# A delta-rule attention and a softplus-erf MLP on one core: a new hand-over order of 3663 operations, and other engines for some copies

## The chip, the core and the metric

The kernel runs on one core of a Trainium2 chip. The metric is the device time of one execution in microseconds, lower is better. Three runs of the kernel before took 779.32, 781.75 and 782.74 us. The profile is of a fourth execution.

## What is computed

The first half is a recurrence over 768 steps with a state of 40 x 40 per head, for 4 x 8 heads. Its output, 3072 tokens of 320 numbers, goes through an MLP of width 2048. All is float32; the weights arrive as float64.

```python
for t in range(S):
    y[:, :, t] = np.einsum('bhd,bhde->bhe', rt, state)
    Sa = np.einsum('bhde,bhe->bhd', state, at)
    state_decay = state * wt[:, :, None, :] - np.einsum('bhd,bhe->bhde', Sa, bt)
    state = state_decay + np.einsum('bhd,bhe->bhde', vt, kt)
...
h = x @ w_in
sp = np.maximum(h, 0.0) + np.log1p(np.exp(-np.abs(h)))
g = h * erf(sp)
return (g @ w_out).astype(np.float32)
```

## The kernel before

The 768 steps are cut into 12 stages of 64, and a stage into two chunks of 32. Stages are counted from 0 here. Each stage has these parts, all heads side by side:

- `prep` (L416) multiplies up the decays w with scans on VectorE (DVE).
- `aphase` (L444), once per chunk: A (L466) multiplies keys by scaled keys, Am (L477) masks the product, and AD writes the part that has to be inverted to DRAM. bT (L485) transposes the keys.
- `tphase` (L490), once per stage: 28 short DVE operations (L512, L513) invert 16 x 16 blocks; TD and tb (both L373) carry the result through DRAM. W and DAD (both L531, 128 small matmuls each on the chip) make the off-diagonal blocks, with the copy Wm between them, and Tb (L538) adds their product into the tile `Tb`.
- `chain` (L540), once per chunk, carries the state on: Z (L571), copy zt, U (L582, which reads `Tb`), copy us, four copies zu of `Us` into `Vu` (L592), the transposes pmt (L599) and UT (L608), copy vtu, PQ (L618), the mask PQm (L621), and MY (M is L632, Y is L636), whose sum gives the new state (MT, L639) and the output (Ym, L641).
- the MLP follows a stage behind: `load_x` (L768) reads the output back and splits it into a high and a low half, mm1 (L802) multiplies by w_in, 8 matmuls to a group of 128 x 256, `unit` (L817) makes the activation on ScalarE (ACT) and DVE, and mm2 (L854) multiplies by w_out, 128 x 320. E and G (L844, L845) give the `h` that mm2 reads.

At the start, 190 warm-up matmuls (L413) write a tile that nobody reads, and `weights` (L700) turns float64 into float32 pairs (L719 to L737).

No loop fixes what runs when. The methods only list operations, each with the keys that it reads and writes, and `Plan.schedule` (L205) returns two tables that stand at the top of the file: `ORDER`, a permutation of the numbers 0 to 3662, and `ENGINES`, one letter for each operation (P TensorE, A ACT, V DVE, S SP, G GpSimd). Operations are handed over in that order, and each engine runs its own in the order handed over.

```python
        for o, e in zip(ops, self.engines):
            o["eng"] = CODE[e]
        return list(self.order)
...
                for i in order:
                    o = N.P.ops[i]
                    N.cur = i
                    o["fn"](o["eng"])
```

Only copies (`copy`, L365, with its lines L367 on ACT and L369 on DVE), fills and the zu copies (L592: ACT, DVE, or a DMA on SP's queue) have a choice of engine. All DMAs are issued in order on SP's queue.

Of the kernel before, what the change touches and what calls it, by code (L numbers as in the profile page):

```python
# [15 lines left out]
17 6 13 10 2 3 4 5 20 210 217 1 457 216 233 232 0 297 435 21 22 23 24 25 26 27 28 29 30 31 32 33 34 35 36 37 38 39 40 41 42 43 44 45 46 47 48 49 50 51  # L16
52 53 54 55 56 57 58 59 60 61 212 211 9 12 8 11 7 219 213 215 218 235 234 62 63 64 65 66 67 68 69 70 71 220 221 72 73 475 74 75 76 77 78 79 224 225
214 298 228 299 300 19 229 18 436 463 464 14 301 80 81 82 230 231 83 84 85 236 237 15 476 240 241 222 223 461 226 306 442 227 243 242 337 441 248 249
86 87 88 89 90 91 92 466 93 94 95 96 97 98 99 100 101 102 103 104 105 106 107 108 109 110 111 244 112 113 114 115 116 302 117 118 119 120 304 121 465
122 123 303 245 252 253 305 307 308 437 309 444 438 440 338 254 255 256 257 258 259 310 124 125 126 246 127 128 129 130 131 132 313 133 134 135 136  # L20
137 138 139 140 477 141 142 143 144 145 146 147 148 311 149 150 151 152 153 154 155 156 315 328 238 359 251 462 346 459 260 316 317 318 261 262 263
264 265 266 329 267 268 269 270 271 272 273 274 275 276 277 278 330 279 280 281 331 443 360 467 339 340 478 319 332 321 312 157 158 159 160 161 162
163 164 165 322 166 167 168 169 170 171 368 250 239 282 283 377 285 284 386 16 247 369 314 370 378 286 347 348 379 349 323 324 172 173 174 175 176 325
333 177 335 178 179 180 181 182 183 184 185 186 187 188 287 288 289 290 291 189 190 191 292 192 293 294 193 295 194 195 196 380 361 362 363 371 387
296 388 389 469 468 445 446 341 327 334 350 326 470 450 449 479 344 197 198 453 199 200 473 480 345 491 509 506 448 458 460 407 395 399 510 490 411
452 481 482 493 396 336 454 472 471 474 483 397 408 409 201 342 455 484 486 485 492 353 524 487 202 354 488 513 489 398 456 352 355 525 343 372 512
203 356 494 495 514 515 516 526 517 518 364 366 358 390 519 498 410 527 499 528 511 497 403 507 451 415 508 501 500 427 496 696 447 547 548 521 404
# [934 lines left out]
```

## Time and profile before

| | |
|---|---|
| median of 3 runs | 781.75 us (779.32 to 782.74) |
| profiled execution, its own time | 776.95 us |
| its span, first to last instruction | 775.2 us |
| granted TensorE clock, mean | 0.973 of full speed |
| busy: TensorE / DVE / ACT / GpSimd | 717.8 / 622.8 / 525.8 / 6.6 us |
| moved by DMA | 93.97 MB, 121 GB/s |
| warm-up matmuls (L413) within TensorE's busy time | 48.3 us |

TensorE's busy time holds matmuls; weight loads (PEld, 573.5 us) overlap them. Busy shares are an average over stages. In the waits of an engine, "issue" means that no semaphore explains the wait. The DMA queues are told by kind; those of kind instruction bring the engines' program, not data.

### The profile page before, as it was taken

To read this page: it belongs to the slowest core of one execution; us is meant where nothing else is said; L and a number is where in the kernel's file an instruction comes from. 1 tells how busy PE (TensorE), PEld (TensorE's weight loads), DVE (VectorE), ACT (ScalarE), POOL (GpSimd) and SP (SyncE) were. 2 spreads that over 40 slices of the span, in tenths; PEclk is the share of its full clock that TensorE was granted. 3 is DMA by queue.
4 is the path that set the end of the run, shared out by engine and by line. 5 is a ranking of instruction groups with operands and counts; after the bars stand their busy time and mean duration, and the time that the engine had idled before them with its cause. 6 is when DMAs were issued, how large, how long until landed. Compare 5 with 4: busy or idle time off the path is not lost.

```text
span 775.2 us, 30880 instructions
## 1 busy us (share of the span) xinstructions
PE 717.8 (93%) x13807; PEld 573.5 (74%) x13807; DVE 622.8 (80%) x1115; ACT 525.8 (68%) x739; POOL 6.6 (1%) x11
## 2 busy tenths in 40 slices
PE   9998788799989999999979989999999999998986
PEld 4556577577877787887867777788788887787863
DVE  7876887797887797888958967878988897678573
ACT  3324456747786697687957667787778885787791
POOL 3000000000000000000000000000000000000000
PEclk9999999999999999999989989999999999999998
DMA  7996776463464563645473662466545643521000
GB/s 193 240 211 189 191 188 150 92 144 97 104 158 91 142 155 68 158 123 115 97 154 75 130 152 62 103 164 150 113 107 125 148 105 94 103 61 41 16 18 21
DMA packets 172480, 93.97 MB, mean 121 GB/s; under 512 B 142484, under 2 KB 154132, under 8 KB 172340
## 3 DMA queue, kind: packets, MB, share of 16 engines
q1 hardware_dynamic: 172340, 91.93, 50.7%
q8 instruction: 110, 1.80, 1.0%
q14 instruction: 30, 0.25, 0.1%
HBM read 73.52 MB, written 14.16 MB: 113 GB/s over the span
## 4 chain that ended last, share of the span: by engine, by line
PE 78%; DVE 9%; issue 5%; DMA 4%; ACT 2%; SPq 1%; DVEq 0%; ACTq 0%
PE po L854 23%; PE ph L802 21%; PE ph L413 6%; PE pA L531 4%; PE my L632 4%; PE pA L466 4%; PE pQ L618 3%; PE my L582 3%; PE pQ L599 2%; PE pA L485 2%; PE my L571 2%; DMA Tb<-TD 2%; PE my L636 2%; PE pQ L608 1%; SPq L373 1%
## 5 line engine op out<-in xcount | busy, mean ns | idle before, releaser
L854 PE MATMUL po<-wo,h 128*128 128x320 f32 x768 | 242.8, 449 | 7.4 <-DVE h L845 6.8
L854 PEld LDWEIGHTS po<-wo,h 128*128 128x128 f32 x768 | 137.1, 193 | 52.3 <-DVE h L845 7.5
L810 ACT ACTIVATE l<-l 128x1024 f32<-128x1024 f32 x96 | 99.1, 1055 | 5.2 <-DVE nd L833 4.6
L802 PE MATMUL ph<-xh,wih 128*128 128x256 f32 x384 | 94.3, 327 | 1.3 <-issue 1.3
L802 PE MATMUL ph<-xh,wil 128*128 128x256 f32 x384 | 78.3, 285 | 0.5 <-issue 0.5
L802 PE MATMUL ph<-xl,wih 128*128 128x256 f32 x384 | 78.2, 286 | 0.0
L802 PEld LDWEIGHTS ph<-xh,wih 128*128 128x128 f32 x384 | 63.1, 194 | 9.8 <-issue 1.7
L367 ACT COPY h<-ph 128x512 f32<-128x512 f32 x74 | 42.7, 584 | 40.3 <-PE ph L802 35.3
L833 DVE TENSOR_TENSOR nd<-l,r 128x1024 f32<-128x1024 f32 x48 | 58.5, 1219 | 5.2 <-ACT r L810 3.6
L802 PEld LDWEIGHTS ph<-xh,wil 128*128 128x128 f32 x384 | 60.8, 194 | 1.4 <-issue 1.4
L802 PEld LDWEIGHTS ph<-xl,wih 128*128 128x128 f32 x384 | 60.6, 194 | 0.0
L834 DVE SCALAR_TENSOR_TENSOR r<-nd,r 128x1024 f32<-128x1024 f32 x48 | 58.4, 1217 | 0.5
L844 DVE TENSOR_TENSOR l<-l,r 128x1024 f32<-128x1024 f32 x48 | 58.2, 1218 | 0.7
L845 DVE SCALAR_TENSOR_TENSOR h<-l,h 128x1024 f32<-128x1024 f32 x48 | 58.3, 1219 | 0.6
L802 PE MATMUL ph<-xh,wir 128*128 128x256 f32 x192 | 54.9, 286 | 2.3 <-DVE xh L369 2.3
L802 PE MATMUL ph<-xl,wir 128*128 128x256 f32 x192 | 55.0, 286 | 0.6 <-issue 0.6
L810 ACT ACTIVATE l<-h 128x1024 f32<-128x1024 f32 x48 | 50.0, 1054 | 0.6 <-DVE h L369 0.2
L810 ACT ACTIVATE r<-l 128x1024 f32<-128x1024 f32 x48 | 49.3, 1052 | 1.6 <-DVE l L844 1.5
L632 PE MATMUL my<-Vu,sg 64*40 64x72 f32 x1536 | 46.4, 230 | 4.1 <-DVE Pr L641 1.4
L810 ACT ACTIVATE r<-r 128x1024 f32<-128x1024 f32 x48 | 49.6, 1056 | 0.4
L413 PE MATMUL ph<-d 104*128 104x512 bf16 x190 | 48.3, 396 | 1.6 <-DVE d L384 1.6
L632 PEld LDWEIGHTS my<-Vu,sg 64*40 64x40 f32 x1536 | 34.9, 115 | 18.2 <-DVE MT L639 4.1
(122 smaller groups left out, 1284.5 us busy)
## 6 DMA issues: line engine op xcount, KB each, us to landing
bk<-in_kba_e SPq DMA_DIRECT2D x48, 416.0 KB
vt<-in_rv_e SPq DMA_DIRECT2D x48, 240.0 KB
h<-in_moe_w_in SPq DMA_DIRECT2D x10, 512.0 KB
h<-in_moe_w_out SPq DMA_DIRECT2D x10, 512.0 KB
Pr<-in_w_e SPq DMA_DIRECT2D x12, 422.9 KB
Rt<-in_r_e SPq DMA_DIRECT2D x24, 208.0 KB
Zm<-in_v_s SPq DMA_DIRECT2D x24, 160.0 KB
Zs<-bk SPq DMA_DIRECT2D x48, 80.0 KB
```

Source lines behind the costliest of these rows:

```text
L367: self.nc.scalar.copy(o, i)
L413: P.add("warm", "PE", lambda e: nc.tensor.matmul(s.ph[1], s.d1[:, :128], s.d1[:, :512], start=True, stop=True), ["d1"], ["phw"], -1e3, 0.22)
L466: nc.tensor.matmul(pa[i % 2 * 64:i % 2 * 64 + 64, i // 4, i // 2 % 2], bk[:, i].rearrange("p a b -> p (a b)"), ab[:, :, i], start=True, st ...
L531: nc.tensor.matmul(pw[js, i, ts], l[js, i], r[js, i, ts], start=True, stop=True)
L632: nc.tensor.matmul(my[h * 64:h * 64 + 40, x, j], sg[xs, g, j, h], vu[xs, g * HQ + j // 2 * 2 + h, j % 2], start=True, stop=False)
L802: nc.tensor.matmul(ph[:, j * 256:j * 256 + 256], a[:k, fs], b[:k], start=(m == 0), stop=(m == 7))
L810: self.P.add(name, "ACT", lambda e: nc.scalar.activation(out=o, in_=i, **kw), rd, wr + ["act"], pr, 1.06)
L833: P.add("nd", [("DVE", 1.2)], lambda e, r=r, l=l, nd=nd: s.eng(e).tensor_tensor(out=nd, in0=l, in1=r, op=ALU.mult), kl + kr, kn, pr)
L834: P.add("rho", "DVE", lambda e, r=r, nd=nd: nc.vector.scalar_tensor_tensor(out=r, in0=nd, scalar=2 * C4, in1=r, op0=ALU.add, op1=ALU.mult) ...
L844: P.add("E", [("DVE", 1.2)], lambda e: s.eng(e).tensor_tensor(out=l, in0=l, in1=r, op=ALU.mult), kr, kl, pr)
L845: P.add("G", "DVE", lambda e: nc.vector.scalar_tensor_tensor(out=h, in0=l, scalar=-1.0, in1=h, op0=ALU.add, op1=ALU.mult), kl, kh, pr, 1.2)
L854: nc.tensor.matmul(po, h[:, bs], s.wo[:, f], start=(f == 0), stop=(f == 15))
```

## The change

Both tables are replaced. The list of operations, their functions and their dependencies stay as they are.

```diff
 ORDER = tuple(int(x) for x in """
-17 6 13 10 2 3 4 5 20 210 217 1 457 216 233 232 0 297 435 21 22 23 24 25 26 27 28 29 30 31 32 33 34 35 36 37 38 39 40 41 42 43 44 45 46 47 48 49 50 51
...
+2 4 3 17 6 7 9 10 12 15 8 5 20 210 1 217 0 216 232 297 435 233 337 457 306 21 22 23 24 25 26 27 28 29 30 31 32 33 475 34 35 36 37 38 39 40 41 42 43 44
...
 ENGINES = "".join("""
-SSVVVVGGGAGGAGAVVGAAPPPPPPPPPPPPPPPPPPPPPPPPPPPPPPPPPPPPPPPPPPPPPPPPPPPPPPPPPPPPPPPPPPPPPPPPPPPPPPPPPPPPPPPPPPPPPPPPPPPPPPPPPPPPPPPPPPPPPPPPPPPPPPPPPPPPPPPP
...
+SSVVVVGGVGGAGAAVVGAAPPPPPPPPPPPPPPPPPPPPPPPPPPPPPPPPPPPPPPPPPPPPPPPPPPPPPPPPPPPPPPPPPPPPPPPPPPPPPPPPPPPPPPPPPPPPPPPPPPPPPPPPPPPPPPPPPPPPPPPPPPPPPPPPPPPPPPPP
...
```

By the second table, the zu copies go from 65 on ACT, 24 on DVE and 7 on SP to 40, 41 and 15. The copies h of mm1's result (L367 on ACT, L369 on DVE) go from 74 and 22 to 80 and 16; the copies of x (`xh`) from 18 and 18 to 12 and 24; those of bT's result from 35 and 13 to 44 and 4. The rest moves by a few.

TensorE in stage 2, from W to the first U, before. `Ti` is W's operand and `Tb` that of DAD and U; a count at the end of a row is of the program's matmuls, and each of L531, L582 and L854 is two on the chip:

```order
L531 MATMUL pA<-Ti,Aw 32x16 x64
L854 MATMUL po_131<-wo,h 128x320 x3
L531 MATMUL pA<-Tb_76,Aw 32x16 x64
L854 MATMUL po_131<-wo,h 128x320
L854 MATMUL po_132<-wo,h 128x320
L466 MATMUL pA<-bk_86 64x2x32 x16
L582 MATMUL my<-zt,Tb_76 32x40 x32
```

The same place now:

```order
L531 MATMUL pA<-Ti,Aw 32x16 x48
L854 MATMUL po_131<-wo,h 128x320
L531 MATMUL pA<-Ti,Aw 32x16 x16
L854 MATMUL po_131<-wo,h 128x320
L531 MATMUL pA<-Tb_76,Aw 32x16 x48
L854 MATMUL po_131<-wo,h 128x320 x2
L531 MATMUL pA<-Tb_76,Aw 32x16 x16
L854 MATMUL po_132<-wo,h 128x320
L582 MATMUL my<-zt,Tb_76 32x40 x32
```

Four rows of L854 now stand inside W and DAD where three stood, and one stands between DAD and U where two stood and A (L466).

TensorE in stage 8, DAD and what follows it, before:

```order
L531 MATMUL pA<-Tb_76,Aw 32x16 x64
L854 MATMUL po_132<-wo,h 128x320
L466 MATMUL pA<-bk_86 64x2x32 x16
L854 MATMUL po_131<-wo,h 128x320
L582 MATMUL my<-zt,Tb_76 32x40 x32
```

DAD of the same stage now:

```order
L531 MATMUL pA<-Tb_76,Aw 32x16 x32
L802 MATMUL ph_129<-xh_0_122,wih_110 128x256
L802 MATMUL ph_129<-xh_1_123,wih_111 128x256
L802 MATMUL ph_129<-xh_2_124,wir 128x256
L802 MATMUL ph_129<-xl_0_125,wih_110 128x256
L802 MATMUL ph_129<-xl_1_126,wih_111 128x256
L802 MATMUL ph_129<-xl_2_127,wir 128x256
L802 MATMUL ph_129<-xh_0_122,wil_112 128x256
L802 MATMUL ph_129<-xh_1_123,wil_113 128x256
L854 MATMUL po_132<-wo,h 128x320 x2
L854 MATMUL po_131<-wo,h 128x320 x2
L531 MATMUL pA<-Tb_76,Aw 32x16 x32
```

A group of mm1 and four rows of mm2 now cut DAD in two halves.

SP's queue in stage 2, where a copy of `Us` into `Vu` is issued, before:

```order
L373 DMA AD_105<-Zs_68 32x16x32
L373 DMA bk_86<-in_kba_e 104x1024
L592 DMA Vu<-Us 32x8x40
L373 DMA xd<-Pr_80 40x4x64 x3
L373 DMA AD_105<-Zs_69 32x16x32 x2
```

In the same stage now:

```order
L373 DMA bk_87<-in_kba_e 104x1024
L373 DMA vt_93<-in_rv_e 40x2x768
L592 DMA Vu<-Us 32x8x40 x2
L373 DMA AD_105<-Zs_68 32x16x32 x2
L373 DMA out<-ob_128 64x320
```

Two such copies are issued one behind the other, and behind them on the queue stand the transfer of the next product to DRAM and a piece of the output.

## Rows read from the trace of the kernel before

**Rows 1.** The page: busy time by engine, and the chain's shares by engine.
```profile
PE 717.8 (93%) x13807; PEld 573.5 (74%) x13807; DVE 622.8 (80%) x1115; ACT 525.8 (68%) x739; POOL 6.6 (1%) x11
...
PE 78%; DVE 9%; issue 5%; DMA 4%; ACT 2%; SPq 1%; DVEq 0%; ACTq 0%
```
**Rows 2.** Waits of TensorE: line, releaser, us in total, times, longest us.
```profile
PE pA L531 <- issue: 17.9, 9, 3.9
PE po L854 <- DVE h L845: 6.8, 6, 2.2
PE my L582 <- issue: 5.3, 5, 2.1
...
PE pQ L608 <- ACT Us L367: 1.9, 3, 0.7
```
**Rows 3.** The page, DMA queues: packets, MB, share of 16 engines.
```profile
q8 instruction: 110, 1.80, 1.0%
```
**Rows 4.** Timeline of TensorE in stage 6: start us, us, instructions, idle before.
```profile
399.09 1.20 PE L531 MATMUL pA<-Tb,Aw 32*32 32x16 f32 x74 [3.91 <-issue]
...
404.35 0.96 PE L582 MATMUL my<-zt,Tb 32*32 32x40 f32 x42
406.15 0.41 PE L582 MATMUL my<-zt,Tb 32*32 32x40 f32 x22 [0.83 <-issue]
```
**Rows 5.** The chain that ended last, in order of time: start us, us, what.
```profile
56.90 3.10 issue
...
104.98 5.02 DMA Tb<-TD
...
115.61 2.73 issue
...
231.16 1.37 issue
...
395.18 3.91 issue
...
400.29 2.00 PE ph L802 x8
402.29 2.13 PE po L854 x4
...
432.84 4.85 PE po L854 x18
...
443.44 4.79 PE ph L802 x40
...
457.16 3.74 issue
...
518.98 1.27 issue
...
698.96 1.28 issue
```
**Rows 6.** Busy time in four stretches: us, engines, granted clock, DMA share, GB/s.
```profile
399.10:406.20 7.10, 6.27 (x132) 4.85 (x135) 2.78 (x3) 0.00 (x0) 0.00 (x0) 0.57 0.44 96
...
452.00:457.00 5.00, 5.00 (x221) 4.76 (x221) 4.81 (x4) 4.97 (x7) 0.00 (x0) 1.00 0.82 192
...
461.00:467.00 6.00, 6.00 (x159) 4.59 (x159) 3.46 (x4) 0.00 (x0) 0.00 (x0) 0.54 0.27 89
...
570.00:575.00 5.00, 4.46 (x196) 3.80 (x185) 4.10 (x4) 4.66 (x7) 0.00 (x0) 1.00 0.14 45
```
**Rows 7.** The tile Tb: its writer on DVE, ns min/median/max.
```profile
L538 DVE TENSOR_TENSOR Tb<-pA,Tb x12: 425/425/426, 60.4 to 685.5; 128x256 f32<-128x256 f32 x12
```
**Rows 8.** Line L592 on ACT, and the timeline from one such DMA to the first M.
```profile
L592 ACT COPY Vu<-Us x65: 453/457/462, 63.4 to 702.4; 32x320 f32<-32x320 f32 x65
...
191.90 0.63 SPq L592 DMA_DIRECT2D Vu<-Us  x1
...
196.20 0.34 PE L632 MATMUL my<-Vu,sg 64*40 64x72 f32 x8
```

More of the change, by code (lines that the diff above doesn't have):

```diff
@@ L156 @@
-PAPVPPVPVVPVVSSSSSSAVPPAPPVAVAAPVPVPAPPVPVVPVVSSSSSSSSVPVVSVVSVVSSVVAAAAAAAAVVVVAAAPPVPPAAPPAPPAAVVPPPPPPPPVVPPPPPPPPVSSVSSAAAAAAAAVVVVAAAPPVPPVAPPVPP
+SSVVVVGGVGGAGAAVVGAAPPPPPPPPPPPPPPPPPPPPPPPPPPPPPPPPPPPPPPPPPPPPPPPPPPPPPPPPPPPPPPPPPPPPPPPPPPPPPPPPPPPPPPPPPPPPPPPPPPPPPPPPPPPPPPPPPPPPPPPPPPPPPPPPPP
+PPPPPPPPPPPPPPPPPPPPPPPPPPPPPPPPPPPPPPPPPPPPPPPPPPPPPPPPPPPPSAVVVVSSVVPPSSVVSSPAPASSVVPPSSVVSSPAPASSSSAAVVVVVVVVVVVVVVVVVVVVVVVVVVVVSSSSVPPPPAPPPPVSVV
+VAPAPVSVVVAPAPASVVVAAAPVVPAVSVVVAPAPVSVVVAPAPASVVVAAAPAAPAVSVVVAPVPASVVVAPAPVSVVVAPVPASVVVAPAPASVVVSVVVSVVVSVVVSVVVSVVVSVVVSVVVSVVVSVVVSAVVVVSSVVPPSSV
@@ new lines @@
+VSSPAPASSSSSSAVPPVPPAAAAAPAPVPAPPVPVVPVVSSVVPPSSVVSSPAPASSSSSSAVPPAPPAAVAVPAPAPAPPVPVVPVVSSSSSSSSSSSSAAVVVVVVVVVVVVVVVVVVVVVVVVVVVVSSSSVPPPPAPPPPVSAVS
+AVSSVVPPAPPAAPPAPPAAAAAAAAAAVVVVAAAPPVPPVAPPAPPAAVVPPPPPPPPVVPPPPPPPPSAVVVVSSVVPPSSVVSSPAPVSSSSSSVVAPPVPPAVVAAPAPAPAPPVPVVPVVSSVVPPSSVVSSPAPASSSSSSVVP
+PAPPAVVAAPVPVPVPPVPVVPVVSSSSSSSSSSSSAAVVVVVVVVVVVVVVVVVVVVVVVVVVVVSSSSVPPPPAPPPPVSAVSVVSSAVAAAAAAAAVVVVAAAPPAPPAAPPAPPAAVVPPPPPPPPVVPPPPPPPPASSASSAAAA
+AAAAVVVVAAAPPAPPAAPPAPPAAVVPPPPPPPPVVPPPPPPPPSAVVVVSSVVPPSSVVSSPAPASSSSSSVAAPPAPPVVASSPAPAPVPPVPVVPVVSSVVPPSSVVSSPAPASSSSSSVAPPAPPAASSVPVPVPAPPVPVVPVV
@@ new lines @@
+SSSSSSSSSSSSAAVVVVVVVVVVVVVVVVVVVVVVVVVVVVSSSSVPPPPAPPPPVSVVSAVSSVVAAAAAAAAVVVVAAAPPVPPAAPPAPPAAVVPPPPPPPPVVPPPPPPPPVSSASSAAAAAAAAVVVVAAAPPAPPAAPPAPPA
+AVVPPPPPPPPVVPPPPPPPPSAVVVVSSVVPPSSVVSSPAPASSSSSSVAVPPAPPAAAVAPAPAPVPPVPVVPVVSSVVPPSSVVSSPAPASSSSSSVAPPAPPAAVAVPVPAPAPPVPVVPVVSSSSSSSSSSSSAAVVVVVVVVVV
+VVVVVVVVVVVVVVVVVVSSSSVPPPPAPPPPVSAVSAVSSVVAAAAAAAAVVVVAAAPPVPPAAPPAPPAAVVPPPPPPPPVVPPPPPPPPASSVSSAAAAAAAAVVVVAAAPPAPPAAPPAPPAAVVPPPPPPPPVVPPPPPPPPSAV
+VVVSSVVPPSSVVSSPAPASSSSSSVAVPPAPPAVAVSPVPAPAPPVPVVPVVSSVVPPSSVVSSPAPVSSSSSSAVPPAPPAVAVVPVPAPAPPVPVVPVVSSSSSSSSSSSSAAVVVVVVVVVVVVVVVVVVVVVVVVVVVVSSSSVP
@@ new lines @@
+PPPAPPPPVSVVSVVSSAVAAAAAAAAVVVVAAAPPVPPAAPPAPPAAVVPPPPPPPPVVPPPPPPPPASSASSAAAAAAAAVVVVAAAPPAPPAAPPAPPAAVVPPPPPPPPVVPPPPPPPPSAVVVVSSVVPPSSVVSSPAPASSSSS
+SVAAPPVPPAAVVAPAPVPAPPVPVVPVVSSVVPPSSVVSSPAPASSSSSSAVPPVPPAVAAAPVPAPAPPVPVVPVVSSSSSSSSSSSSAAVVVVVVVVVVVVVVVVVVVVVVVVVVVVSSSSVPPPPAPPPPVSVVSAVSSVVAAAAA
+AAAVVVVAAAPPAPPAAPPAPPVAVVPPPPPPPPVVPPPPPPPPASSVSSAAAAAAAAVVVVAAAPPAPPAAPPVPPAAVVPPPPPPPPVVPPPPPPPPSAVVVVSSVVPPSSVVSSPAPASSSSSSVAAPPAPPASVVSPAPVPAPPVP
+VVPVVSSVVPPSSVVSSPAPASSSSSSAVPPAPPAVVVSPAPAPAPPVPVVPVVSSSSSSSSSSSSAAVVVVVVVVVVVVVVVVVVVVVVVVVVVVSSSSVPPPPAPPPPVSVVSVVSSAVAAAAAAAAVVVVAAAPPAPPAAPPAPPAA
@@ new lines @@
+VVPPPPPPPPVVPPPPPPPPASSASSAAAAAAAAVVVVAAAPPVPPAAPPAPPAAVVPPPPPPPPVVPPPPPPPPSAVVVVSSVVPPSSVVSSPAPASSSSSSVVVPPAPPAVVAAPVPAPAPPVPVVPVVSSVVPPSSVVSSPAPASSS
+SSSVVPPAPPAVAVAPVPVPAPPVPVVPVVSSSSSSSSSSSSAAVVVVVVVVVVVVVVVVVVVVVVVVVVVVSSSSVPPPPAPPPPVSVVSVVSSVVAAAAAAAAVVVVAAAPPAPPAAPPAPPAAVVPPPPPPPPVVPPPPPPPPASSA
+SSAAAAAAAAVVVVAAAPPVPPAAPPAPPAAVVPPPPPPPPVVPPPPPPPPSAVVVVSSVVPPSSVVSSPAPASSSSSSVAAPPVPPASVSVPAPVPAPPVPVVPVVSSVVPPSSVVSSPAPVSSSSSSAAPPAPPVAVAVPAPAPAPPV
+PVVPVVSSSSSSSSSSSSAAVVVVVVVVVVVVVVVVVVVVVVVVVVVVSSSSVPPPPVPPPPVSVVSVVSSVVAAAAAAAAVVVVAAAPPAPPAAPPAPPAAVVPPPPPPPPVVPPPPPPPPASSASSAAAAAAAAVVVVAAAPPAPPAA
@@ new lines @@
+PPAPPAAVVPPPPPPPPVVPPPPPPPPSAVVVVSSVVPPSSVVSSPAPASSSSSSVAAPPVPPAAVSSPVPAPAPPVPVVPVVSSVVPPSSVVSSPAPASSSSSSVAPPAPPAVAVAPVPAPAPPVPVVPVVSSSSSSSSSSSSAAVVVV
+VVVVVVVVVVVVVVVVVVVVVVVVSSSSVPPPPAPPPPVSVVSAVSSVVAAAAAAAAVVVVAAAPPAPPAAPPAPPAAVVPPPPPPPPVVPPPPPPPPVSSASSAAAAAAAAVVVVAAAPPAPPAAPPAPPAAVVPPPPPPPPVVPPPPP
+PPPSAVVVVSSVVPPSSVVSSPVPASSSSSSVVAPPAPPAAAASPVPAPVPPVPVVPVVSSVVPPSSVVSSPAPASSSSSSVVPPAPPAASSAPAPAPAPPVPVVPVVSSSSSSSSSSSSAAVVVVVVVVVVVVVVVVVVVVVVVVVVVV
+SSSSVPPPPAPPPPVSVVSVVSSVVAAAAAAAAVVVVAAAPPAPPAAPPAPPAAVVPPPPPPPPVVPPPPPPPPVSSVSSAAAAAAAAVVVVAAAPPAPPVAPPVPPAAVVPPPPPPPPVVPPPPPPPPSSSSSSVAVPPAPPAVVVVPV
@@ L157 @@
+PVPAPPVPVVPVVSSSSSSVAPPAPPAAAVVPAPAPVPPVPVVPVVSSSSSSSSVPVVSVVSAVSSVVAAAAAAAAVVVVAAAPPVPPAAPPAPPAAVVPPPPPPPPVVPPPPPPPPVSSVSSAAAAAAAAVVVVAAAPPVPPVAPPVPP
 VAVVPPPPPPPPVVPPPPPPPPAAAAAAAAVVVVAAAVVPPPPPPPPVVPPPPPPPPASSASS
```

23 lines of the change are left out of this document (removed), and 228 rows, old and new, of the table ORDER.

## Prediction

> **What bounds the kernel now.** I read first the busy times and the chain that ended last. The reader is to see that TensorE is busy for 717.8 of 775.2 us and carries 78% of the chain [rows 1], so what matters is what stops TensorE. The chain's next shares are DVE with 9% and "issue" with 5%, and issue is time in which the engine waited for nothing that the profile shows.
>
> Then the waits of TensorE [rows 2]. The longest total is no dependency: L531 sat 17.9 us behind "issue", in 9 waits of up to 3.9 us, and L582 5.3 us in 5. All waits for VectorE's h at L845 are 6.8 us together. The table of DMA queues has one queue of kind instruction with 110 packets and 1.80 MB, about 16 kB each [rows 3]. TensorE runs 13807 matmuls and as many weight loads [rows 1], so one such packet serves about 251 instructions. The timeline shows the same grain: between the wait that ends at 399.09 and the one that ends at 406.15 stand 74, 8, 4 and 42 matmuls [rows 4, 5], 128 matmuls with their 128 weight loads, 256 instructions. So I read these waits as the end of a block of 256 instructions whose successor has not arrived. They fall on L531 because its matmuls are the smallest: 74 take 1.20 us [rows 4], while 18 of L854 take 4.85 us and 40 of L802 take 4.79 us [rows 5].
>
> A page speaks against such waits. The Trainium skill, "Runtime: NRT & Kernel Launch", section "Instruction fetch mechanics", has blocks of 256 instructions fetched during the one before, and calls the crossing "mostly hidden". The size agrees with the trace, the hiding doesn't at the tiny matmuls; by that rule the change would gain nothing.
>
> Two more things decide the size of a wait. In the 5 us before the 3.74 us wait at 457.16 the DMA engines were busy at 0.82; around the same place of stage 9, 570 to 575, they were at 0.14 and TensorE worked 4.46 of the 5 us [rows 5, 6]. So a load seems late when data fills the engines. And the granted clock falls behind a long wait: 0.57 over the 7.1 us from 399.1 and 0.54 over the 6 us from 461 [rows 6]; 8 matmuls of L802 then take 2.00 us and 4 of L854 2.13 us [rows 5], where the full-clock rows give 8 x 4.79/40 = 0.96 and 4 x 4.85/18 = 1.08.
>
> **The change, part by part.** Every transfer, matmul and vector operation is still there, so TensorE's own work is unchanged. What moves is the filler between the small matmuls. One group of L802 (8 rows of the order) costs 0.96 us. One row of L854 is two matmuls on the chip, 2 x 4.85/18 = 0.54 us. I counted both in all stages 1 to 11.
>
> (a) Between the first W and the last DAD (both L531) there stood 25 groups of L802 and 14 rows of L854, 24.0 + 7.6 = 31.6 us. Now there are 27 and 31, 25.9 + 16.7 = 42.6 us, 1.0 us more per stage. A wait shrinks at most by the filler added. Stage 1 waits 2.73 us and gains one group: 0.96. Stage 3 waits 1.37 and gains one row: 0.54. Stage 6 waits 3.91 and gains one group and one row: 1.50. Stage 8 waits 1.27 and gains three rows, 1.62: all 1.27. The waits of L531 besides the six listed make 17.9 - (3.10 + 2.73 + 1.37 + 3.91 + 3.74 + 1.27) = 1.8 us [rows 2, 5], in stages that gain at least as much: 1.8. Together 6.1. Stage 7 goes the other way: of its three groups two now stand inside W, ahead of the block that runs out, so its 3.74 us may grow by 2 x 0.96 = 1.9. Stage 0 has warm-up matmuls as filler; I leave it at nothing. Net 4.2 us off, bounds 2 (one of the gains more fails) and 6.1 (stage 7 does not grow).
>
> (b) The filler came mostly from behind DAD. Before the second U (L582) there stood 20 rows of L854, now 10: 5.4 us less. There L538 must add DAD's product to Tb, 425 ns each [rows 7], so the one row that is left (0.54) just hides it. But U has block ends of its own, 5.3 us [rows 2]. Bounds 0 (hidden) and 5.4 (every microsecond reappears); I take 2: of those waits one shows in stage 6 right after DAD, at 406.15 [rows 4], and it can grow by the 0.96 that left there; one more stage like it makes 2.
>
> (c) The half clock cost (2.00 - 0.96) + (2.13 - 1.08) = 2.1 us in stage 6, and I price stage 7 alike. Bounds 0 and 4.2; I take 2, since only stage 6's wait is cut.
>
> (d) Block ends elsewhere, such as the 1.28 us at 698.96 [rows 5], get a little more or less filler. At 698.96 one group of L802 now stands before the end. Bounds -1 and +3; I take 1.5 off.
>
> (e) Copies change engine. Of L592's 96, ACT loses 25 (25 x 0.457 = 11.4 us), DVE gains 17 and SP 8 [rows 8]. DVE loses others to ACT, six h copies at L367 among them. ACT has 249 us to spare and DVE 152 [rows 1]; TensorE waits for ACT's Us 1.9 us in all [rows 2], so I cost this at nothing. Its cover is the UT, PQ and mask between Us and the first M: a DMA issued at 191.90 had until 196.20 [rows 8]. Behind these DMAs on SP's queue stand transfers like AD and out, which TensorE needs a stage later or not at all.
>
> The sum is -4.2 + 2 - 2 - 1.5 = -5.7 us. The profiled execution took 776.95 us, below the median of the three runs, 781.75; from it the sum gives 771.2, and on the median's scale, which I forecast, **776.0 us**.
>
> **The rivals.** *No change.* The waits only move behind DAD. All 5.4 us of (b) come back as waits of U and nothing is won on the clock: -4.2 - 1.5 + 5.4 = -0.3, so 781.5. For it: the sum of TensorE's work is the same and the loads must still arrive. Against: the two longest waits, 3.91 and 3.74, both stand inside L531, where the filler goes. The Trainium skill's rule ("Runtime: NRT & Kernel Launch", "Instruction fetch mechanics"), by which such loads are mostly hidden, would end here too, with nothing to gain and 781.75 us. Half a per cent is about what a measurement of this kernel can tell, 3.9 us.
>
> *Slower.* The copies handed to SP arrive late. SP has 15 of them where it had 7, some in pairs. The cover is 4.3 us [rows 8]; a small transfer in the chain, Tb's, took 5.02 us [rows 5]. With 0.63 us of issue, 5.02 + 0.63 - 4.3 = 1.35 us per copy, 8 copies: 11 us slower, less 5.7: 787. It decides once a landing takes over 3.7 us. Against: TensorE shows no wait at L632 for such a DMA, with 7 of them.
>
> *Much faster.* Filler ends nearly all waits of L531 and the half clock with them: 17.9 + 4.2 = 22 us, 760. Against: in stage after stage DAD and U still run down a block in under 4 us, and loads behind busy DMA engines take longer than the filler.
>
> **How the numbers follow.** Forecast 0.50, no change 0.33, slower 0.13, much faster 0.04. Faster by over 0.5% (under 777.8) is the forecast's case for the most part, plus the last: 0.53. Within 0.5%: 0.33. Slower (over 785.7): 0.14. The low end takes all good bounds, -6.1 - 4.2 - 3 = -13.3, and 2 us of spread as the runs show (779.32 to 782.74): 766. The high end takes the bad bounds, -2 + 5.4 + 1 = +4.4, which is 786; I put it at 785, and most of the slower case stays outside.
>
> **What would show it.** Right: L531's issue waits under 14 us, the longest under 3, no half clock in stage 6, L802 and L854 unchanged in length. Wrong: L531 still near 18 us or L582 above 9 us (no change), or waits at L632 ended by a DMA of Us (slower). If the whole falls by 10 us or more with the issue waits unchanged, the copies' engines were the reason, and step (e) failed.

## The result, and the profile after

The changed kernel took **790.9 us** (median of 4 runs, 788.86 to 801.27), the kernel before 781.0 us beside it (4 runs, 779.32 to 782.74): ratio 1.0118, 95% interval 1.0077 to 1.0159. Forecast were 776.0 us and a range of 766 to 785. The forecast missed, on the slower side. Later the change was timed twice more, twelve runs each: 783.2 us beside 783.5 (ratio 0.9948, 0.9900 to 0.9995) and 782.1 us beside 784.3 (ratio 0.9998, 0.9951 to 1.0044). So the loss of the first four runs did not return, and no gain showed in both repeats: the first is half a per cent faster, the second level. Ratios leave out disturbed runs; medians take all.

The first profiled run of the change spans 787.8 us. Its page:

```profile
PE 730.6 (93%) x13807; PEld 581.7 (74%) x13807; DVE 625.0 (79%) x1131; ACT 515.0 (65%) x715; POOL 6.1 (1%) x10
...
PE 67%; DVE 13%; DMA 8%; issue 6%; ACT 4%; SPq 2%; DVEq 0%; ACTq 0%
```

Against [rows 1], the work on DVE and ACT shifted as the table of engines says (ACT -10.8 us, DVE +2.2). TensorE's matmuls are the same 13807, and yet they took 12.8 us more: busy time grew, idle time (57.2 us after, 57.4 before) did not. Nearly all of this is lost early. Up to the first W of stage 3 the busy time of about 3646 matmuls was 199.5 us before and is 212.0 now, and that W comes at 233.9 us instead of 224.1. Stage 1 shows it best, before and after (stretch, its length, busy time of PE, PEld, DVE, ACT and POOL, granted clock, DMA share, GB/s):

```profile
111.50:171.60 60.10, 49.25 (x1096) 41.72 (x1096) 49.83 (x89) 40.44 (x56) 0.00 (x0) 0.94 0.58 132
```
```profile
113.00:176.00 63.00, 56.99 (x1099) 48.49 (x1099) 49.02 (x89) 40.13 (x54) 0.00 (x0) 0.78 0.49 111
```

Nearly as many matmuls took 7.7 us longer at a granted clock of 0.78 instead of 0.94. The chain went in part from TensorE to DVE and DMA. TensorE's waits, in the same view as [rows 2]:

```profile
PE pA L531 <- issue: 8.3, 7, 1.6
PE my L582 <- issue: 5.9, 6, 2.0
PE po L854 <- DVE h L845: 5.1, 4, 2.5
PE my L571 <- DVE Ti L513: 4.2, 1, 4.2
PE po L854 <- issue: 4.1, 2, 2.7
PE pA L531 <- DVE Ti L521: 4.0, 3, 2.0
...
PE my L632 <- DMA Vu<-Us: 1.6, 2, 1.1
```

The waits on "issue" are called block waits from here on, since the kept traces bear out how the prediction read them. Each of the twelve that last 0.8 us or more in the trace of before ends 1.28 to 1.55 us after a packet of the instruction queue has landed. Counted over TensorE's matmuls, weight loads and sequencer instructions, each ends at the same place of a count of 256 (192 or 193).

L531's block waits fell from 17.9 to 8.3 us, the longest from 3.9 to 1.6, as the forecast asked (in two later profiles the longest was 4.4 and 3.8). But L854 now waits 4.1 us for blocks, and L632 waits for a DMA of Us, which it did not before. Stage 6 on the timeline, to be held against [rows 4]:

```profile
409.50 0.99 PE L531 MATMUL pA<-Tb,Aw 32*32 32x16 f32 x96
410.43 0.81 PE L854 MATMUL po<-wo,h 128*128 128x320 f32 x2
411.16 0.49 PE L582 MATMUL my<-zt,Tb 32*32 32x40 f32 x32
...
412.32 0.33 PE L582 MATMUL my<-zt,Tb 32*32 32x40 f32 x11
414.47 0.41 PE L582 MATMUL my<-zt,Tb 32*32 32x40 f32 x21 [1.83 <-issue]
414.81 2.27 PE L854 MATMUL po<-wo,h 128*128 128x320 f32 x4
```

The wait of 3.91 us inside L531 is gone. One of 1.83 us stands in U, behind it, and four L854 rows after it take 2.27 us, where four at full clock take 1.08: the half clock follows this wait too (0.58 granted from 414.5 to 418 us).

### The profile page after: what moved, and what is told of

The parts are those of the page before. It is cut to its first block, busy times and chain, and to the rows that moved or that the text cites. A ratio compares the mean times of both kernels' runs of the same rounds, so it can differ in the third digit from the quotient of the medians.

```text
span 787.8 us, 30869 instructions
## 1 busy us (share of the span) xinstructions
PE 730.6 (93%) x13807; PEld 581.7 (74%) x13807; DVE 625.0 (79%) x1131; ACT 515.0 (65%) x715; POOL 6.1 (1%) x10
## 4 chain that ended last, share of the span: by engine, by line
PE 67%; DVE 13%; DMA 8%; issue 6%; ACT 4%; SPq 2%; DVEq 0%; ACTq 0%
PE po L854 19%; PE ph L802 18%; PE my L632 4%; PE ph L413 4%; PE pA L531 4%; PE pA L466 3%; PE pQ L618 3%; PE my L582 3%; PE pA L485 2%; SPq L373 2%; PE my L571 2%; PE pQ L599 2%; PE my L636 2%; DMA TD<-Ti 1%; DMA h<-in_moe_w_in 1%
## 5 line engine op out<-in xcount | busy, mean ns | idle before, releaser
L854 PE MATMUL po<-wo,h 128*128 128x320 f32 x768 | 245.9, 450 | 9.2 <-DVE h L845 5.1
L854 PEld LDWEIGHTS po<-wo,h 128*128 128x128 f32 x768 | 135.9, 193 | 50.1 <-DVE h L845 7.1
L802 PE MATMUL ph<-xh,wih 128*128 128x256 f32 x384 | 95.7, 331 | 0.8 <-ACT zt L367 0.6
L802 PE MATMUL ph<-xl,wih 128*128 128x256 f32 x384 | 78.7, 287 | 1.8 <-issue 1.3
L802 PE MATMUL ph<-xh,wil 128*128 128x256 f32 x384 | 78.4, 286 | 0.4 <-issue 0.4
L802 PEld LDWEIGHTS ph<-xh,wih 128*128 128x128 f32 x384 | 63.6, 194 | 11.1 <-issue 0.9
L367 ACT COPY h<-ph 128x512 f32<-128x512 f32 x80 | 46.6, 583 | 31.5 <-PE ph L802 27.1
L802 PEld LDWEIGHTS ph<-xl,wih 128*128 128x128 f32 x384 | 60.7, 194 | 2.2 <-issue 1.5
L802 PEld LDWEIGHTS ph<-xh,wil 128*128 128x128 f32 x384 | 60.9, 195 | 0.6 <-issue 0.6
L802 PE MATMUL ph<-xh,wir 128*128 128x256 f32 x192 | 55.0, 286 | 0.5 <-DVE xh L369 0.5
L632 PE MATMUL my<-Vu,sg 64*40 64x72 f32 x1536 | 48.3, 234 | 7.3 <-DMA Vu<-Us 1.6
L802 PE MATMUL ph<-xl,wir 128*128 128x256 f32 x192 | 55.0, 286 | 0.0
L632 PEld LDWEIGHTS my<-Vu,sg 64*40 64x40 f32 x1536 | 35.8, 117 | 22.9 <-DVE Vu L621 8.4
```

Of the source, the lines that this page charges most:

```text
L367: self.nc.scalar.copy(o, i)
L632: nc.tensor.matmul(my[h * 64:h * 64 + 40, x, j], sg[xs, g, j, h], vu[xs, g * HQ + j // 2 * 2 + h, j % 2], start=True, stop=False)
L802: nc.tensor.matmul(ph[:, j * 256:j * 256 + 256], a[:k, fs], b[:k], start=(m == 0), stop=(m == 7))
L854: nc.tensor.matmul(po, h[:, bs], s.wo[:, f], start=(f == 0), stop=(f == 15))
```

## The experiments

Eighteen runs were made in five sessions, each beside the kernel before, whose median in them was 782.2, 783.5, 784.3, 783.8 and 783.9 us. The sums "of the waits view" below add all rows of that view: those ended by "issue" (block ends), and those ended by another engine or a DMA.

**Order or engines alone.** The change has two tables. e1 takes ENGINES alone from the change, e2 ORDER alone; e4 and e5 splice the two kernels at the first W of stage 3 (e4: before's first part, e5: the change's), both tables. The beginnings of the first rows that differ, in ENGINES and in ORDER:

```diff
-SSVVVVGGGAGGAGAVVGAAPPPP
+SSVVVVGGVGGAGAAVVGAAPPPP
...
```
```diff
-17 6 13 10 2 3 4 5 20 210 217 1 457 216 233 232 0 297 435 21
+2 4 3 17 6 7 9 10 12 15 8 5 20 210 1 217 0 216 232 297 435 233
...
```

> The order of the kernel before with the copy engines of the change. Theory A (the new copy engines cost the time: 15 copies of Us into Vu on SP's queue instead of 7, more copies of x and of Sm on DVE): slower than before by 5 us or more, near 787, and TensorE's waits at L632 grow as in the change. Theory B (the new order costs it): within 3 us of before, 778 to 784.

> The order of the change with the copy engines of the kernel before. Theory A (engines): within 3 us of before. Theory B (order): slower than before by 7 us or more, 788 to 793, with the issue waits of L531 still near 8 us.

> Order and engines of the kernel before up to the first W of stage 3, those of the change from there. Theory C (the loss is made at the start, stages 0 to 2, where the change's profile reaches W of stage 3 9.8 us late): within 3 us of before, 778 to 784. Theory D (the loss is spread over the steady stages): slower by 5 us or more.

> Order and engines of the change up to the first W of stage 3, those of the kernel before from there. Theory C (start): slower than before by 7 to 10 us, 788 to 791, with more than 30 us at half clock before 160 us. Theory D (steady stages): within 4 us of before.

Measured: e1 896.3 us (1.150, 1.142 to 1.157), e2 868.8 (1.111, 1.105 to 1.117), e4 786.2 (1.001, 0.997 to 1.006), e5 781.6 (0.996, 0.991 to 1.001). Nobody expected 11 to 15%. Their largest new waits, TensorE of e1 and then of e2:

```profile
PE pA L485 <- DVE Zs L477: 13.2, 4, 10.0
```
```profile
PE po L854 <- ACT ob L367: 10.1, 3, 7.3
```

Copies come late in many places: TensorE waits 105.7 and 96.1 us for engines and DMA, where before it waited 22.8. Here each order is good with its own engine table only. Theories A and B, by which one table carried the loss, both fall. Neither half of the change costs what the whole had cost in its first four runs: e5 speaks against theory C, and e4, 4 us over before by its median and level by its ratio, settles nothing between C and D.

**The change and before again.** No edit.

> The change itself, timed again in five rounds. Theory C (the whole is dearer by more than its two halves, because what the start loses isn't won back): about 790 us, ratio near 1.012. Theory N (the halves show that nothing measurable was lost, and the first four runs of the change were on the long side of a spread of 775 to 790 us that the kernel before itself has): 782 to 785 us, ratio 1.000 to 1.005. In the profile both expect the waits of L531 for an instruction block near 8 us (17.9 before), and the starts of stages 0 to 2 tell them apart: the first W of stage 3 at 233.9 us again by theory C, at 226 to 230 us by theory N.

> The kernel before against itself: ratio 1.000, with an interval that says how small a difference these rounds can tell. Its second profile tells how steady the two things are that are read as causes: theory M (the waits at block ends belong to the order) expects L531 to wait 16 to 19 us for its blocks again, in 8 to 10 waits; theory D (they are drawn anew in each execution) expects a sum that differs by more than 4 us, with waits at other stages. The half clock, about 41 us of the span in the first profile, comes out within 7 us by M and not by D.

> The change a third time, five rounds, beside before. So far: 790.9 us against 781.0 in four runs, then 783.2 against 783.5 in twelve; over all runs timed 0.01 of granted clock went with 7 us, and at one clock (0.965) the change stood at 788 both times and before at 781 to 784. Theory H (the change loses some 5 us by waits on copies, and the half clock is drawn anew in each execution and covers or doubles that): at one clock again 4 to 6 us over before, with a median between 782 and 791 us according to the clock it draws. Theory Q (the change also keeps the clock up, 0.971 against 0.963 last time, because its block waits are shorter): a mean clock over 0.968 again, median 781 to 785 us.

Measured: 783.2, 785.1 and 782.1 us (r2's ratio 0.9973, 0.9926 to 1.0020). r1 and r3 come near theories N and Q without meeting either in full: r1's ratio lies under N's range, and r3's mean clock was 0.967 where Q asked for more than 0.968. Five profiled runs of the two programs:

| | span, us | clock | first W of stage 3 at | from there to the end | PE busy | waits, issue | waits, engines and DMA |
|---|---|---|---|---|---|---|---|
| before | 775.2 | 0.973 | 224.1 | 551.1 | 717.8 | 28.0 | 22.8 |
| before again | 784.5 | 0.954 | 233.0 | 551.5 | 726.0 | 30.4 | 21.5 |
| change | 787.8 | 0.956 | 233.9 | 553.9 | 730.6 | 23.5 | 25.3 |
| change again | 780.2 | 0.972 | 232.1 | 548.1 | 721.4 | 22.6 | 27.9 |
| change, third | 776.7 | 0.974 | 225.7 | 551.0 | 720.7 | 21.4 | 26.0 |

The two right columns differ by kernel: the change waits 4.5 to 9 us less for blocks and 2.5 to 6.4 us more for engines and DMA. Where block waits fall is partly drawn anew in each execution: L531 had 17.9 us of them in 9 waits before, and 23.0 in 12 in before again, as r2's theory D expects.

The clock varies between executions of one program, which spans 775.2 or 784.5 us. Stages 0 to 2 take 224 to 234 us with either kernel, at granted clocks there of 0.97, 0.92, 0.91, 0.93 and 0.96 in the order of the table; from stage 3 on the two kernels are level, 551.3 us before and 551.0 after in the mean. In r1's twelve runs the time goes from 774.7 us at a mean clock of 0.982 to 794.5 at 0.955, 7 us for each 0.01. A straight line through these twelve gives 793.1 us at 0.9585, the mean clock of the first four runs; their mean time was 793.0. At 0.965 such lines put the change at 788.1 and 785.7 us (r1, r3) and before beside it at 783.8 and 783.3: at one clock the change is 2 to 4 us slower by this estimate, and it came out level at mean clocks of 0.971 and 0.967 beside 0.964 and 0.965.

Where the clock is lost can be seen in stage 0, first before, then before again (columns as in stage 1 above):

```profile
55.00:60.00 5.00, 1.90 (x119) 1.30 (x115) 2.91 (x6) 2.76 (x6) 0.00 (x0) 1.00 0.99 264
60.00:65.00 5.00, 5.00 (x116) 3.78 (x116) 2.32 (x4) 0.92 (x3) 0.00 (x0) 0.66 0.98 292
65.00:70.00 5.00, 5.00 (x80) 3.83 (x82) 4.06 (x8) 3.27 (x8) 0.00 (x0) 1.00 0.58 156
```
```profile
55.00:60.00 5.00, 1.96 (x33) 0.81 (x37) 0.63 (x2) 1.58 (x4) 0.00 (x0) 0.77 1.03 315
60.00:65.00 5.00, 2.89 (x118) 1.84 (x111) 0.00 (x0) 1.55 (x4) 0.00 (x0) 0.50 0.66 185
65.00:70.00 5.00, 5.00 (x112) 3.64 (x112) 1.88 (x4) 0.88 (x2) 0.00 (x0) 0.50 0.35 106
```

Its block waits, on the timeline of TensorE:

```profile
58.04 0.29 PE L531 MATMUL pA<-Ti,Aw 32*32 32x16 f32 x5 [3.57 <-issue]
...
64.88 0.39 PE L531 MATMUL pA<-Tb,Aw 32*32 32x16 f32 x11 [2.11 <-issue]
```

In the first execution one block is late there (3.10 us, [rows 5]); in the second two are, and the clock stays at its half level into the third stretch. Stage 1 then began 5.5 us later (117.0 against 111.5 us), with the same instructions in the same order. That accounts for one pair of profiles. Why all four first runs of the change drew clocks of 0.956 to 0.964 stays open; the twelve of r1 drew 0.955 to 0.982.

**TensorE's order alone (f1), and SP's (hS, fS).** f1 rearranges only TensorE's own rows from W to the second U of stages 1 to 11, in the sequence of the change; hS takes only SP's sequence; fS both. f1 is not the change's filler: between the first W and the last DAD it has 23 groups of L802 and 19 rows of L854, 32.3 us at the prediction's prices, against 31.6 before and 42.6 in the change. Before U it leaves 6 rows of the 20. So it does not test step (a). First rows that differ in f1:

```diff
-612 585 702 618 422 674 677 619 620 635 586 587 636 588 589 638 385 637
+612 585 702 618 422 674 677 619 620 635 586 587 588 589 636 385 637
...
```

> Before, with TensorE's own order alone rearranged between the first W and the second U of stages 1 to 11, as the change has it; the order of every other engine and all copy engines are those of before. By the prediction's step (a) the longer filler between W and DAD takes 8 to 10 us out of L531's waits for blocks and gives 4 to 5 back in work, so 776 to 780 us, ratio 0.993 to 0.998. The rival (the filler is tuned to the engines' order, so TensorE now waits for copies that come later than it asks) expects waits of L531, L571 and L854 on VectorE and ScalarE to grow by more than the block waits shrink: 785 us and more, ratio above 1.004.

> Before, with the order of SP's queue alone (the issues of the transfers) taken from the change. Theory T (the waits of L531 are loads of instruction blocks held up by bulk transfers that SP issued just before, so SP's order sets them): L531's waits for blocks fall from 18 to 23 us to 12 or less, and the time to 776 to 781 us. Theory F (the filler that TensorE has there sets them): they stay at 16 us or more, and the time is that of before or, if SP's queue now waits in front of a transfer that is wanted, 785 to 800 us.

> Both single parts together: TensorE's order between W and the second U as in the change (791 us alone, with block waits of L531 at 16 us still) and SP's order of the change. Theory J (the waits fall only when filler and transfers move together, as in the change): L531's block waits at 8 to 11 us, and a time below that of either part alone by 3 us or more. Theory A (the parts add): the time of the TensorE part alone plus what SP's order alone gives or costs, within 4 us.

Measured: f1 790.9 us (1.0100, 1.0036 to 1.0164), hS 854.3 (1.091), fS 864.6 (1.101). TensorE's waits between 180 and 700 us, before, the change, and f1:

```profile
PE pA L531 <- issue: 11.7, 6, 3.9
PE my L582 <- issue: 3.2, 4, 1.2
```
```profile
PE my L582 <- issue: 5.4, 5, 2.0
PE pA L531 <- issue: 5.0, 5, 1.4
PE po L854 <- issue: 4.1, 2, 2.7
```
```profile
PE pA L531 <- issue: 8.5, 5, 4.5
PE my L582 <- issue: 5.3, 5, 2.3
PE my L632 <- issue: 2.3, 3, 1.9
```

In this stretch all block waits sum to 18.4 us before (19.7 again), 18.1 in f1, and 18.3, 16.1 and 14.1 in the change: they move out of L531 to what comes behind, L582, L632 and L854, and little goes away. The rest of what the change saves at block ends lies outside this stretch, from 9.6 and 10.7 us to 5.2, 6.5 and 7.3. Waits for other engines and DMAs rise from 3.2 us (3.2 again) to 7.8 in f1 and 7.3, 8.6 and 7.1 in the change. In f1 that fits the rival of its expectation, by which TensorE asks in an order that the copies were not made for; but its mean clock was 0.959 beside 0.964, about half of its loss at 7 us for each 0.01. In hS L531 still waits 14.5 us for blocks, between its two theories. In fS it waits 9.4 us, as theory J asks, while the time is within 4 us of the sum of the parts, as theory A asks. Neither answers the question, since SP's queue in the foreign order blocks what is wanted next, and TensorE waits 71.6 and 81.4 us for engines and DMA. Two such waits in hS:

```profile
PE my L632 <- DMA Vu<-in_v_x: 15.7, 6, 7.6
...
PE my L632 <- DVE Vu L621: 9.0, 2, 8.6
```

**The copies of L592 alone.** e3 is the change with these copies on before's engines, e7 is before with them on the change's. A piece of e7's row:

```diff
-SSAVPPAPPAAVAAPVPVPAPPVPVV
+SSAVPPAPPAAVAVPVPVPAPPVPVV
...
```

> The change with the engines of the L592 copies (Us) alone set back to those of before (65 on ScalarE, 24 on VectorE, 7 by SP instead of 40, 41 and 15). By the prediction's step (e) these cost nothing: within 0.5% of the change itself. By its slower rival the eight more copies by SP land too late and L632 waits for a DMA of Us (2.7 us more idle time of PE and its loads in the change): 3 to 6 us less than the change. By the theory that order and engines are one tuned pair, found with the two whole tables each tried alone (869 and 896 us), even 25 or so copies on another engine than the order was made for cost: 5 to 30 us more than the change.

> Before with the engines of the L592 copies alone taken from the change (ScalarE 65 to 40, VectorE 24 to 41, SP 7 to 15), all orders kept. The prediction's step (e) says nothing, within 3 us of before. The theory that order and engines are one pair (setting these copies back in the change cost it 18 us) says 8 to 25 us over before, with new waits of L632 on the Us copies.

Measured: e3 801.6 us, 18 more than the change beside it (1.0167, 1.0062 to 1.0271, against before); e7 831.4 (1.0610, 1.0519 to 1.0701). The pair theory's direction holds both times; e3 lies in its range, and e7's 47 us lie far above its 8 to 25, at a mean clock of 0.938 beside 0.965. The new waits are not mainly the ones that it named, of L632 on the Us copies, but these in e7 (of SP, then of DVE, then of TensorE), against SP of before in the last fence:

```profile
SPq L592 <- ACT Us L367: 33.9, 5, 16.7
SPq L592 <- ACT Vu L592: 30.5, 2, 16.8
...
DVE bk L459 <- DMA bk<-in_kba_e: 12.6, 3, 10.7
...
PE pA L485 <- DVE Zs L477: 14.3, 4, 10.6
```
```profile
SPq L592 <- ACT Vu L592: 14.4, 3, 6.8
...
SPq L592 <- ACT Us L367: 9.9, 4, 3.9
```

A copy given to SP makes SP's queue wait at L592, up to 16.8 us at a time, and loads of bk land late; DVE then waits up to 10.7 us for bk. In the change SP waits 59.8 us at L592 in all (25.2 before, 79.4 in e7) without such waits of DVE; that its order has room for this is likely but not shown. e3 shows the other side: with the copies on the engines of before, TensorE waits for ACT's Sm and for a load of Vu:

```profile
PE my L632 <- DMA Vu<-in_v_x: 5.5, 2, 3.8
...
PE pQ L608 <- ACT Sm L367: 4.7, 1, 4.7
```

**Where the block ends fall.** Tiny matmuls whose results are overwritten shift every block end behind them; all orders and engines are kept. `PAD` holds counts by operation. By the traces the first W of every stage then stands at 157 or 158, 89 or 90, and 244 or 245 of its block, as planned.

```diff
-            P.add("warm", "PE", lambda e: nc.tensor.matmul(s.ph[1], s.d1[:, :128], s.d1[:, :512], start=True, stop=True), ["d1"], ["phw"], -1e3, 0.22)
+            P.add("warm", "PE", lambda e, k=PAD.get(len(P.ops), 0): [nc.tensor.matmul(s.ph[1][:a, :b], s.d1[:, :a], s.d1[:, :b], start=True, stop=True) for a, b in [(32, 1)] * k + [(128, 512)]], ["d1"], ["phw"], -1e3, 0.22)
...
-            def mm(e, f=f, j=j):
-                fs = slice(f * 128, f * 128 + 128)
+            def mm(e, f=f, j=j, pad=PAD.get(len(P.ops), 0)):
+                fs = slice(f * 128, f * 128 + 128); [nc.tensor.matmul(ph[:32, j * 256:j * 256 + 2], s.wih[0][:, f * 128:f * 128 + 32], xh[0][:, :2], start=True, stop=True) for _ in range(pad)]
```

> Before, with 382 tiny matmuls (32 columns of weights, 1 or 2 moving columns, results overwritten) put in front of L413 and L802 work, so that in every stage the first W stands at instruction 158 of its 256-instruction block (in before it stands at 11, 129, 28, 230, 182, 133, 111, 70, 49, 11, 245, 161). Profiles so far show little waiting at block ends where W stood at 133 to 182 (0 to 1.3 us in a stage, once 2.0) and most at 4 to 11 in stage 0 and at 70 to 129 (2 to 5 us). Theory P (where the block ends fall against the stretch of short matmuls decides the waits): L531 waits 8 us or less for blocks, all block ends together 15 us or less (some 30 before), mean clock up, and 770 to 779 us in spite of some 5 us for the added matmuls. Theory B (busy transfer engines decide, wherever the ends fall): 25 us or more at block ends still, and 785 to 792 us.

> The same with 348 tiny matmuls, so that W stands at 90 in every stage, among the places that showed the most waiting. Theory P: 30 to 45 us at block ends, a lower clock, 795 to 815 us. Theory B: as with W at 158, within 4 us.

> The same with 426 tiny matmuls, so that W stands at 245 in every stage; only stage 10 of before stood there, and it did not wait. Theory P: as at 158, L531 at 8 us or less and 770 to 780 us; if that one stage stayed clear for another reason (its transfers), 785 to 800 us. Theory B: as with 158 and 90.

> The change with 373 tiny matmuls, W at 158 in every stage. The change waits less for blocks to begin with (25 to 28 us at all block ends against 32), by the longer filler between W and DAD. Theory P: 15 us or less at block ends, 774 to 782 us, a gain below that of before with W at 158, since the filler had already taken part of it. Theory B: 785 to 792 us.

Measured: 809.4, 803.4, 844.1 and 828.1 us (ratios 1.033, 1.024, 1.047, 1.055). Times alone mislead here, since the padding in stage 0 cost far more than planned. The sums of block waits say more: 25.5, 32.9 and 28.4 us on before, where it had 28.0 and 30.4; between 180 and 700 us 15.1, 19.9 and 21.8. Theory P asked for 15 or less at 158 and 245 against 30 to 45 at 90; only the last came. On the change the padding made them longer, 33.9 us where it had 21.4 to 23.5, and 26.6 between 180 and 700 us where it had 14.1 to 18.3. So no place tried brings the waits to what theory P asks, and place still matters by up to 10 us, in a way that neither theory gives. TensorE waited in k158, in k90, and in k158 on the change:

```profile
PE pA L531 <- issue: 13.3, 7, 4.5
PE my L582 <- issue: 7.0, 9, 1.4
```
```profile
PE my L582 <- issue: 14.1, 10, 4.3
PE pA L531 <- issue: 13.8, 4, 4.2
```
```profile
PE pA L531 <- issue: 17.9, 7, 5.6
```

**Lighter transfers.** From stage 3 on four loads bring a few partitions only (m1 on before, m2 on the change); what the two compute from there on is not the reference's result.

```diff
-        s.dma("zv", lambda: zm[64:96].rearrange("p g a b e -> p (g a b e)"), lambda: I["v_s"][ck], wr=[("zm", "v")], pr=prl)
+        zk = 32 if ck < 6 else 2; s.dma("zv", lambda: zm[64:96].rearrange("p g a b e -> p (g a b e)")[:zk], lambda: I["v_s"][ck][:zk], wr=[("zm", "v")], pr=prl)
...
```

> Before, but from stage 3 on four kinds of loads (vt, Rt, Zm and Vu inputs, some 2.0 MB of a stage) bring a thirteenth of their partitions or fewer, with the issues, orders and waits kept: the values computed from stage 3 on are not the reference's. Stages 3 to 11 of before wait 21.6 us at block ends in the first profile and 21.7 us in the second. Theory B (bulk transfers hold up the loads of instruction blocks): 12 us or less there, L531 a quarter of what it was, and a time of 755 to 770 us with the half clock going too. Theory O (a block of short matmuls is simply over before the next load can be done, however free the transfer engines are): 18 us or more still, and 772 to 782 us.

> The change with the same loads cut from stage 3 on. Stages 3 to 11 of the change wait as long at block ends (22.6 and 21.4 us in two profiles) as those of before, in other places. Theory B: 12 us or less here too, and a time of 755 to 770 us. Theory O: 18 us or more. If the change's longer filler between W and DAD is worth anything once loads are free, it ends below m1 by 3 us or more; if the waits only moved, within 3 us of m1.

Measured: m1 761.8 us (0.9807, 0.9728 to 0.9887), m2 769.0 (0.9891, 0.9849 to 0.9933). The stretch of 180 to 700 us, before and m1 (columns as in stage 1 above), and its longest block waits, m1 and m2:

```profile
180.00:700.00 520.00, 497.06 (x10451) 409.28 (x10451) 430.72 (x775) 387.30 (x540) 0.00 (x0) 0.98 0.51 117
```
```profile
180.00:700.00 520.00, 505.09 (x10891) 416.86 (x10890) 445.27 (x794) 402.78 (x557) 0.00 (x0) 1.00 0.37 85
```
```profile
PE pA L531 <- issue: 4.6, 5, 2.2
PE my L582 <- issue: 3.5, 4, 1.4
```
```profile
PE pA L531 <- issue: 5.1, 5, 1.9
PE my L582 <- issue: 2.4, 4, 0.8
```

With the DMA share down from 0.51 to 0.37, all block waits there fall from 18.4 us to 10.6 (m1) and 10.7 (m2, where the change had 14.1 to 18.3), and the clock of m1 in that stretch rounds to 1.00. From the first W of stage 3 on, the stretch that the expectations speak of, the waits view gives 19.7 and 18.7 us for the two profiles of before, 16.5, 15.7 and 14.1 for the change, 10.2 for m1 and 9.7 for m2. (The 22.6 and 21.4 us that m2's expectation gives for the change are sums over the whole execution.) So transfers that fill the DMA engines hold up the loads, as theory B says; about half of the block waits stay, with L531 at 4.2 of 11.7 us rather than a quarter. The trace of m1 shows a reason for what stays, in the sense of theory O: the load of a block begins 0.9 us after the block before it has begun (median; in 79% of cases after, not ahead of it), takes 1.1 us, and no block starts less than 1.2 us after its load has landed. By these numbers a load needs some 3.2 us from there (an estimate), while 128 matmuls of L531 alone, a whole block, run in 1.26 us.

The waits are not the whole gain: from that W on m1 takes 531.7 us where before took 551.1, 9.5 less at block ends, 1.5 less for engines and DMA and 8.7 less in TensorE's busy time, at a clock of 0.99 against 0.97. With lighter loads the change is 7.2 us slower than m1 by medians, outside both cases of m2's expectation, and its filler saves nothing (10.7 against 10.6 between 180 and 700 us). What makes it slower is not shown: from stage 3 on m2's profile is 7.7 us longer, 5.4 of it in TensorE's busy time, and its waits for engines and DMA are 6.3 us against 5.4.

No kernel that computes the right result was clearly faster than before: e5 (781.6 us) and the change (782 to 783) are level with it.

## Why the prediction was wrong, step by step

Two steps failed. (c) counted on 2 us from the clock, and in the profile of the first four runs the same matmuls took 12.8 us more; (e) put the copies' new engines at nothing, and waits for engines and DMA grew by some 4 us. The case that came closest is the rival that was given a third: no change, the waits move behind DAD, 781.5 us. The repeated runs lie at 782 to 783. The first four, at 790.9, lie in the range of the slower case (over 785.7) and beyond its 787, but only by chance: its mechanism, TensorE waiting 11 us for the copies by SP, was there with 1.6 us.

(a) Filler in W to DAD, -4.2: the direction was right and, for L531 alone, the size too small. Between 180 and 700 us L531's block waits went from 11.7 (15.6 again) to 5.0, 5.2 and 4.0 us. Stage 7, forecast to grow by 1.9, fell from 3.74 to a wait of 1.39 us in the chain, now at L854. "A wait shrinks at most by the filler added" was no bound; that m1 shortens the waits without any filler shows one reason, the transfers around a load.

(b) Less filler before the second U, +2: mis-sized. All block waits outside L531 in that stretch were 6.7 us (4.1 again) and became 13.3, 10.9 and 10.1: about +6, by the bound that the prediction had named ("every microsecond reappears", 5.4) and not taken. It looked at U alone, which took a quarter of it (L582 from 3.2, 1.9 again, to 5.4, 3.8 and 3.3); L854 took nearly half (from 0.6 to 4.1, 2.9 and 3.0), and L466 and L632 most of the rest. f1 shows a like exchange for TensorE's order alone, with hardly more filler: L531 at 8.5 and the others at 9.6 us.

(c) Half clock, -2: the step that decided the first four runs. It priced the clock by two waits, in stages 6 and 7, and left stages 0 to 2 at nothing. There the profile of those runs has 12.5 of the 12.8 us by which TensorE's busy time grew, at a granted clock of 0.91 against 0.97, while its idle time did not grow. Before again lost 7.2 us of busy time there as well, at 0.92. The clock is no property of the order that could be counted on: the mean of the change was 0.959, 0.971 and 0.967 in its three sessions, that of before 0.961 to 0.966 in five. At 7 us for each 0.01 the change's alone swings by some 8 us, four times the term. The half level did leave stage 6's L531 and came back behind U. What set the clock of the first four runs stays open.

(d) Other block ends, -1.5: cannot be told apart from (b) in these sums. The 1.28 us at 698.96 is out of the chain; two of 1.26 us are in it later.

(e) Copies change engine at no cost: the step that failed in kind. "ACT has 249 us to spare and DVE 152" is true and says nothing of when a copy runs. Waits for engines and DMA rose by some 4 us (22.8 and 21.5 before; 25.3, 27.9 and 26.0 after). How much of that is the engines and how much the new order is not shown: e3 and e7 show that the L592 copies cannot be costed apart from the order, being 18 us better on their new engines in the new order and 47 us worse in the old. L632's new wait on a DMA of Us, the slower rival's sign, was there, at 1.6 us instead of 11.

Put together by waits, the means of the table: block ends 29.2 to 22.5 us, -6.7; engines and DMA 22.2 to 26.4, +4.2; net -2.5 us, against repeated medians 0.3 and 2.2 us below before. The -6.7 stand for (a), (b) and (d), which the forecast put at -3.7 together: (a) and (b) were both too small, and that they offset each other in part is luck. (e) took 4.2 us back, and the 2 us of (c) did not come.

The rule that the prediction set against itself, the Trainium skill's "Runtime: NRT & Kernel Launch", "Instruction fetch mechanics", that crossings are mostly hidden, names the outcome of the repeated runs but not its reason: crossings cost 21 to 30 us here in the five profiles of the two kernels. They are paid elsewhere, not hidden.

## What to carry over

A wait that belongs to a resource, here the loads of instruction blocks behind full DMA engines, can move to the next instructions when filler moves; price it at what all its waits sum to, and attack the resource. In this searched schedule the order and the engine table are one object: no copy that changes engine is free because its engine has idle time, least of all on SP's queue, which issues in order. And where one program spans 775 or 785 us with the clock that it draws, four runs beside four can miss by a per cent, with an interval that does not show it.

## What the runs showed that was not expected

- One more late block in stage 0 went with a longer run at half clock, and the next stage began 5.5 us later (the two profiles of before above).
- Tiny matmuls are not tiny among large ones. With 39, 73 and 117 of them in stage 0 the first W moved from 52.92 us to 61.25, 67.58 and 101.38, 0.2 us each in the first two (k90, k158) and 0.4 in the third (k245). Here are ten matmuls of k245, tiny ones mixed with 512-column warm-ups (0.36 us each), and the 52 warm-ups of before (0.26 us). In k245 the ordinary matmuls around them were longer too up to some 65 us (four of L485 took 0.90 us, in before 0.52), though its profile gives a granted clock of 1.00 there. Why was not tried.

```profile
35.21 3.55 PE L413 MATMUL ph<-d 104*32 104x1 bf16 x10
```
```profile
1.64 13.42 PE L413 MATMUL ph<-d 104*128 104x512 bf16 x52 [1.64 <-DVE d L384]
```
